# Hash attention and RWKV channel mix on one core: first blocks' differences in three pieces, staged weights scaled ten slots behind their loads

## The chip, the core and the metric

The kernel runs on one core of a Trainium2 chip. A core has engines that run side by side, each working through its own instructions in order: TensorE (PE) multiplies matrices out of SBUF into PSUM, and its weight loads are shown apart as PEld; VectorE (DVE), ScalarE (ACT) and GpSimd (POOL) do elementwise work; SyncE (SP) issues most of the transfers, and POOL and ACT issue a few. Engines wait for each other through semaphores. The metric is the device time of one execution in microseconds (us), as a median over several runs.

## What is computed

Two parts follow each other. First, attention over 4 batches of 8 heads, 768 positions, head size 64, in which a query sees only the keys whose six sign bits (of a projection) equal its own. Its output, heads side by side, is the input x of an RWKV channel mix of width 512 and inner width 1024:

```
q_bits = (einsum('bhsd,dk->bhsk', q, proj) > 0)
k_bits = (einsum('bhsd,dk->bhsk', k, proj) > 0)
mask = q_bucket[:, :, :, None] == k_bucket[:, :, None, :]
scores = where(mask, scale * matmul(q, k.transpose(0, 1, 3, 2)), -1e9)
x = matmul(softmax(scores), v)
x_prev = concatenate([zeros, x[:, :-1, :]], axis=1)
xk = mu_k * x + (1.0 - mu_k) * x_prev
xr = mu_r * x + (1.0 - mu_r) * x_prev
k = maximum(xk @ w_k, 0.0)
v = k * k @ w_v
r = 1.0 / (1.0 + exp(-(xr @ w_r)))
out = r * v
```

## The kernel before

**Pairs and slots.** Heads are taken two at a time: 16 pairs n, four for each batch (NPB is 4). A pair has 12 slots, one for each head j of the two and each of six blocks of 128 keys. One loop over the global slot G (line 605) writes the order of all engines by hand; n and s are the pair and the slot in it. In every slot PE makes one block of scores (`score`, two matmuls at L325), ACT takes the exponential of it (L332), and PE multiplies the block of two slots before with the values (`pv`, L352). After six blocks DVE divides by the row sums (rc at L363, ob at L364).

**What else a pair's slots hold.** `bits` (slot 1): PE's eight sign-bit matmuls for pair n+1 (L287), DVE's signs sg (L291), and eight small SP transfers (L297) that put the bits beside q and k. `turn_out` (slot 3): PE transposes ob of pair n-1 (L378), DVE copies it to a tile xt (L379), and L383 and L384 set the 128 columns ahead of it, which make xt shifted by one position; POOL does these two, except for the last pair of a batch, where DVE does. `mix(b, dc, 0)` (slot 4): DVE makes the difference df of xt and its shifted self (L394), multiplies it by mu_k (L398) and adds the shifted part (L405); the result xk is 128 of the 512 channels of the channel mix's input. `turn` (slots 5, 7, 9 and 11): PE transposes a quarter of q and k of pair n+2 (L269) into a PSUM bank; DVE empties the bank (L272 for q, L274 for k) and casts the lower half (L278), POOL casts the upper half (L277). The quarters of slots 5 and 9 share one bank, with the sign bits of slot 1, and those of slots 7 and 11 the other, with the transposes of slot 3. `values` (slots 6 and 10): POOL casts v of pair n+1 (L305) and sums it (L311 to L315).

**Loads.** In slot 3 SP issues q and k of pair n+3 (L238) and v of pair n+2 (L248). The channel mix's weights come in during pairs 0 to 2 by the table `weights` (line 587). w_k and w_r are loaded by POOL's own transfers (L537), w_r in slot 10 of pairs 1 and 2. w_v is loaded by SP in four blocks of 512 KB (`load_wv`, L544) into a staging pool of two buffers, in slots 0 and 2 of pairs 1 and 2, and POOL scales each block by one half into the bfloat16 weights wv_sb (L550). The third and the fourth block take the buffers of the first and the second.

**Delays.** `later(k, fn)` enters a function that `run_due`, at the head of each slot, runs k slots on. The scale of a block is entered 8 slots behind its load, which puts it at the head of slots 8 and 10 of the same pair.

**The channel mix.** Its matmuls (L424) come from a queue that `ffn` empties little by little between the scores, from slot 5 of pair 4 on for batch 0; the last batch runs alone at the end. It needs all four xk of a batch first, wr_sb later, and wv_sb last.

Of the kernel before, what the change touches and what calls it, by code (L numbers as in the profile page):

```python
# [10 lines left out]
BF16 = mybir.dt.bfloat16  # L11
INT32 = mybir.dt.int32
AF = mybir.ActivationFunctionType
ALU = mybir.AluOpType
AX = mybir.AxisListType

P = 128
# [12 lines left out]
def kernel(  # L30
# [13 lines left out]
    nc = tc.nc  # L44
    B, H, S, D = q.shape
# [5 lines left out]
    NDC = DM // P  # L51
    NFC = DF // P
    NPB = H // 2
# [18 lines left out]
    mu_sb = consts.tile([P, 2 * NDC], FP32, name="mu_sb")  # L72
# [95 lines left out]
    def fast():  # L168
        with ExitStack() as fx:
# [17 lines left out]
            dfp = pool("df", 1)  # L187
            mixp = pool("mix", 2)
# [7 lines left out]
            def bank(which, shape, dt, name):  # L196
                return bkp.tile(shape, dt, name=name, tag=f"bk{which}")
# [16 lines left out]
            def later(k, fn):  # L214
                due.append((clock[0] + k, len(due), fn))

            def run_due():
                ready = sorted(x[:2] for x in due if x[0] <= clock[0])
                for key in ready:
                    fn = next(x for x in due if x[:2] == key)  # L220
                    due.remove(fn)
                    fn[2]()
# [4 lines left out]
            def load_qk(n, split=False, eng=nc.sync):  # L227
                b, t = divmod(n, NPB)
                tag = f"qk{n}" if n < NKEEP else f"qk{n % 3 - 3}"
                tl = nat.tile([P, 2, 2, S // 2], FP32, name=f"qk{n}", tag=tag)  # L230
                nats[n] = tl
                if split:
                    for j in range(2):
                        for (side, i, src), e in zip(SIDES, (nc.sync, nc.scalar)):
                            e.dma_start(out=tl[:, i, j, :], in_=natural(src, b, 2 * t + j))
                else:
                    for side, i, src in SIDES:
                        eng.dma_start(  # L238
                            out=tl[:, i, :, :],
                            in_=src[b, 2 * t : 2 * t + 2].rearrange(  # L240
                                "j (p c) d -> p j (c d)", c=NC_
                            ),
                        )

            def load_v(n):
                b, t = divmod(n, NPB)
                vf = vfp.tile([P, 2, S // 2], FP32, name=f"vf{n}", tag="vf")
                nc.sync.dma_start(  # L248
                    out=vf, in_=v[b, 2 * t : 2 * t + 2].rearrange("j (p c) d -> p j (c d)", c=NC_)
                )  # L250
                vfs[n] = vf
# [134 lines left out]

            mx = {}

            def mix(b, dc, i):
                xt = xts[b, dc]  # L390
                x, xp = xt[:, P : P + S], xt[:, 0:S]
                if i == 0:
                    df = dfp.tile([P, S], BF16, name=f"df{b}_{dc}", tag=f"df{dc}")
                    nc.vector.tensor_tensor(df, x, xp, op=ALU.subtract)  # L394
                    mx["df", b, dc] = df
                nm = ("xk", "xr")[i]
                m = mixp.tile([P, S], BF16, name=f"{nm}{b}_{dc}", tag=f"{nm}{dc}")
                nc.vector.tensor_scalar(  # L398
                    out=m,
                    in0=mx["df", b, dc],  # L400
                    scalar1=mu_sb[:, i * NDC + dc : i * NDC + dc + 1],
                    scalar2=None,
                    op0=ALU.mult,
                )
                nc.vector.tensor_tensor(out=m, in0=m, in1=xp, op=ALU.add)  # L405
                mx[nm, b, dc] = m

            ffbanks = ["C", "D"]
            ffnext = [0]
# [114 lines left out]
            def ffn(amount):  # L524
                if not queue:
                    credit[0] = 0.0
                    return
                credit[0] += amount
                while queue and credit[0] > 0:
                    cost, u = queue.pop(0)  # L530
                    credit[0] -= cost
                    u()


            def load_w(which, c0, nch):
                dst, src = {"k": (wk_sb, moe_w_k), "r": (wr_sb, moe_w_r)}[which]
                nc.gpsimd.dma_start(  # L537
                    out=dst[:, c0 : c0 + nch, :],
                    in_=src[c0 * P : (c0 + nch) * P, :].rearrange("(c p) f -> p c f", p=P),
                )  # L540

            def load_wv(c0):
                st = stg.tile([P, 2, DM], FP32, name=f"wvs{c0}", tag="stg")
                nc.sync.dma_start(  # L544
                    out=st,
                    in_=moe_w_v[c0 * P : (c0 + 2) * P, :].rearrange("(c p) f -> p c f", p=P),
                )
                later(
                    8,
                    lambda: nc.gpsimd.tensor_scalar(  # L550
                        out=wv_sb[:, c0 : c0 + 2, :], in0=st, scalar1=0.5, scalar2=1.0,
                        op0=ALU.mult, op1=ALU.mult,
                    ),
                )
# [9 lines left out]
            for _ in range(22):  # L564
# [10 lines left out]
                out=mu_rows[0:NDC, :], in_=moe_mu_k.rearrange("(c p) -> c p", p=P)  # L575
            )
            nc.sync.dma_start(
                out=mu_rows[NDC : 2 * NDC, :], in_=moe_mu_r.rearrange("(c p) -> c p", p=P)
# [20 lines left out]
            def oo_bank(n, j):  # L599
                return "AC"[j] if n < NPB else "A"  # L600

            def misc_bank(n, s):
                return "BD"[(s // 2) % 2] if n < NPB else "B"

            for G in range(nslots + LAG):
                clock[0] = G
                n, s = divmod(G, 12)
                live = G < nslots
                run_due()

                if live and s == (5 if n == 0 else 3):
                    if n + 3 < NPAIRS:
                        load_qk(n + 3)
                    if n + 2 < NPAIRS:
                        load_v(n + 2)
                w = weights.get(n, {}).get(s)
                if w:
                    if w[0] == "v":
                        load_wv(w[1])
                    else:  # L620
                        load_w(*w)
                old = chunks[G - LAG] if G >= LAG else None
                first = old is not None and old[2] == 0
                if live:
                    score(*chunks[G])
                if old and not first:
                    pv(*old, oo_bank(*old[:2]))
                rate = 25.9 / (NPB * 12 + (3 if n >= NPAIRS - NPB else 0))
                ffn(rate / 2)
                mb = misc_bank(n, s)  # L630
                if live:
                    if n == 0:
                        if s in (0, 1):
                            turn(1, s, 1, "BD"[s])
                    if n == 1 and s == 0:
                        mups = bank(mb, [P, 2 * NDC], FP32, "mups")
                        nc.tensor.transpose(mups, mu_rows, ident32[0 : 2 * NDC, 0 : 2 * NDC])
                        nc.vector.tensor_copy(mu_sb, mups)
                    if s == (3 if n == 0 else 1) and n + 1 < NPAIRS:
                        bits(n + 1, (0, 1), mb)  # L640
                    if s == 3 and n >= 1:
                        turn_out(n - 1, mb)
                    if s == 4 and n >= 1:
                        mix((n - 1) // NPB, (n - 1) % NPB, 0)

                    if n in (NPB, NPB + 1) and G - NPB * 12 in (7, 9, 11, 13):
                        mix(0, (G - NPB * 12 - 7) // 2, 1)
                    if n > NPB and s == 8:
                        mix((n - 1) // NPB, (n - 1) % NPB, 1)
                    if s in (5, 7, 9, 11) and n + 2 < NPAIRS:  # L650
                        x = (s - 5) // 2
                        turn(n + 2, x % 2, x // 2, mb)
                    if s in (6, 10) and n + 1 < NPAIRS:
                        values(n + 1, s // 10)
                    if s in (8, 10) and NKEEP <= n + 1 < NPAIRS:
                        norm(n + 1, (s - 8) // 2)
                ffn(rate / 2)
                if old and first:
                    pv(*old, oo_bank(*old[:2]))
                if live and n >= NPB and n % NPB == 0 and s == MIXSLOT - 1:  # L660
                    queue.extend(ffn_items(n // NPB - 1))

            nm = sgp.tile([P, 1], FP32, name="nm", tag="nm")
# [32 lines left out]
            x = 0  # L696
# [143 lines left out]
    with tc.manual_schedule():  # L840
        fast()
# [33 lines left out]
```

## Time and profile before

| what | value |
|---|---|
| median of 3 runs | 283.14 us (282.72 to 283.64) |
| the profiled execution | 281.45 us |
| its span, first to last instruction | 279.6 us |
| mean granted clock of TensorE | 0.988 |
| busy PE, ACT, DVE, POOL | 262.2, 215.0, 198.6, 113.3 us |
| DVE's sum of waits for POOL's L384 | 6.9 us in 10 waits |
| PE's waits for DVE's L272 | 1.7 us, one wait |

The costliest groups of the page that the change's steps touch or stand beside (operation, its operands and count; then busy time and the mean of one; then the engine's idle time just before, and what ended most of it):

```profile
L332 ACT ACTIVATE pt<-sc,expb 128x768 bf16<-128x768 f32 x192 | 166.5, 904 | 39.4 <-PE sc L325 38.1
L277 POOL CAST aq<-tq 64x384 bf16<-64x384 f32 x32 | 21.1, 658 | 63.3 <-DVE tq L272 63.3
L272 DVE COPY tq<-tpq 128x384 f32<-128x384 f32 x32 | 17.7, 552 | 2.1 <-PE tpq L269 2.0
L384 POOL COPY xt<-xt 128x127 bf16<-128x127 bf16 x12 | 3.6, 302 | 46.4 <-DVE xt L379 46.4
```

And the instructions on the tile wvs (durations are least, median and most, in ns):

```profile
L544 SPq DMA_DIRECT2D wvs<-in_moe_w_v_dram x4: 386/432/578, 24.2 to 42.1; - x4
L550 POOL TENSOR_SCALAR wv_sb<-wvs x4: 1033/1036/1044, 33.4 to 48.0; 128x1024 bf16<-128x1024 f32 x4
```

The duration at L544 is that of issuing a transfer, not of the transfer. An engine that is not the bottleneck loses nothing by standing idle, as POOL does before most of its casts at L277.

### The profile page before, as it was taken

What the parts mean: (1) busy time and instruction counts of PE and PEld (TensorE: products, weight loads), DVE (VectorE), ACT (ScalarE), POOL (GpSimd) and SP (SyncE); (2) the same over time, 40 slices, a digit from 0 to 9 for tenths busy, and PEclk for the clock granted to TensorE, in tenths of its full rate; (3) what the DMA queues carried; (4) which work ended last, traced back from release to release, by engine and by line L of the source; (5) the groups of instructions that cost most, each with busy time, mean ns of one, the idle gap of its engine ahead of it and who ended that gap; (6) DMA issues with size and microseconds to landing.
All of it is one profiled execution on the core that took longest, in us unless ns stands there. A gap on an engine that the chain in (4) does not pass through costs nothing.

```text
span 279.6 us, 6894 instructions
## 1 busy us (share of the span) xinstructions
PE 262.2 (94%) x2530; PEld 165.4 (59%) x2561; DVE 198.6 (71%) x438; ACT 215.0 (77%) x318; POOL 113.3 (41%) x300
## 2 busy tenths in 40 slices
PE   7999997899999999999999999999999889989991
PEld 5466765666565665656565765656565556545540
DVE  3766839879997866769698766769698835576541
ACT  2199995898799896878989896878998898449800
POOL 5885667665554350714455260715444600000000
PEclk9999997999999999999999999999999999999997
DMA  7459597253213050726122040815220001320042
GB/s 231 167 115 208 179 328 248 43 173 101 77 59 117 6 172 4 218 110 191 59 69 108 14 164 7 272 53 166 84 60 4 5 2 39 114 76 2 0 151 86
DMA packets 19896, 29.95 MB, mean 107 GB/s; under 512 B 2184, under 2 KB 15056, under 8 KB 19856
## 3 DMA queue, kind: packets, MB, share of 16 engines
q1 hardware_dynamic: 17928, 25.89, 27.9%
q0 software_dynamic: 1536, 3.15, 5.3%
q8 instruction: 22, 0.36, 0.5%
q10 hardware_dynamic: 392, 0.40, 0.5%
q14 instruction: 18, 0.15, 0.2%
HBM read 24.12 MB, written 6.29 MB: 109 GB/s over the span
## 4 chain that ended last, share of the span: by engine, by line
PE 66%; ACT 9%; DVE 8%; DMA 7%; issue 3%; SPq 3%; POOL 2%; ACTq 0%; DVEq 0%
PE sc L325 15%; PE vp L424 13%; PE kp L424 12%; PE oo L352 8%; ACT pt L332 6%; PE rp L424 5%; DMA wvs<-in_moe_w_v_dram 4%; PE bb L287 4%; PE tpq L269 3%; PE tpk L269 2%; SPq L297 2%; PE ot L378 2%; ACT sq L256 2%; PE oo L343 1%; DMA aq<-sg 1%
## 5 line engine op out<-in xcount | busy, mean ns | idle before, releaser
L332 ACT ACTIVATE pt<-sc,expb 128x768 bf16<-128x768 f32 x192 | 166.5, 904 | 39.4 <-PE sc L325 38.1
L325 PE MATMUL sc<-aq,ak 70*128 70x384 bf16 x384 | 94.9, 328 | 3.2 <-ACT pt L332 0.8
L352 PEld LDWEIGHTS <-pt 128*128 128x128 bf16 x1152 | 61.1, 98 | 26.6 <-issue 0.8
L352 PE MATMUL oo<-va,pt 128*128 128x65 bf16 x1152 | 66.9, 194 | 0.0
L424 PE MATMUL kp<-xk,wk_sb 128*128 128x384 bf16 x256 | 57.7, 325 | 0.8 <-DVE os L487 0.8
L325 PEld LDWEIGHTS <-ak 70*128 70x128 bf16 x384 | 34.9, 98 | 29.3 <-issue 9.1
L424 PE MATMUL vp<-wv_sb,k 128*128 128x512 bf16 (+1 forms) x186 | 50.3, 370 | 0.4 <-issue 0.2
L277 POOL CAST aq<-tq 64x384 bf16<-64x384 f32 x32 | 21.1, 658 | 63.3 <-DVE tq L272 63.3
L455 DVE TENSOR_TENSOR k<-kr 128x384 bf16<-128x384 bf16 x64 | 29.0, 459 | 15.5 <-ACT kr L447 14.3
L424 PEld LDWEIGHTS <-wk_sb 128*128 128x128 bf16 x256 | 22.2, 97 | 13.3 <-issue 4.2
L256 ACT ACTIVATE sq<-qk 128x768 bf16<-128x768 f32 x32 | 27.1, 847 | 0.1
L424 PE MATMUL rp<-wr_sb,xr 128*128 128x512 bf16 x79 | 24.9, 379 | 1.2 <-DVE kr L449 0.8
L424 PEld LDWEIGHTS <-k 128*128 128x128 bf16 x200 | 17.5, 97 | 12.0 <-issue 2.7
L447 ACT ACTIVATE kr<-kp 128x384 bf16<-128x384 f32 x36 | 17.7, 491 | 7.4 <-PE kp L424 7.4
L487 DVE SCALAR_TENSOR_TENSOR os<-th,vp 128x512 f32<-128x512 bf16 (+1 forms) x25 | 16.5, 663 | 9.0 <-PE vp L424 8.9
L384 POOL COPY xt<-xt 128x127 bf16<-128x127 bf16 x12 | 3.6, 302 | 46.4 <-DVE xt L379 46.4
L311 POOL TENSOR_TENSOR s<-vf 128x192 f32<-128x192 f32 x32 | 20.8, 650 | 0.0
L277 POOL CAST ak<-tk 64x384 bf16<-64x384 f32 x32 | 19.3, 602 | 2.4 <-DVE tk L274 2.4
L274 DVE TENSOR_SCALAR tk<-tpk 128x384 f32<-128x384 f32 x32 | 17.6, 550 | 3.4 <-PE tpk L269 3.3
L272 DVE COPY tq<-tpq 128x384 f32<-128x384 f32 x32 | 17.7, 552 | 2.1 <-PE tpq L269 2.0
L269 PE MATMUL tpq<-ident,qk 128*128 128x128 f32 x96 | 16.9, 287 | 2.4 <-DVE tq L272 1.7
L379 DVE COPY xt<-ot 128x768 bf16<-128x768 bf16 x16 | 8.9, 558 | 14.3 <-PE ot L378 14.2
(60 smaller groups left out, 320.0 us busy)
## 6 DMA issues: line engine op xcount, KB each, us to landing
vf<-in_v_dram SPq DMA_DIRECT2D x16, 384.0 KB
out_dram<-os SPq DMA_DIRECT2D x23, 256.0 KB
qk<-in_q_dram SPq DMA_DIRECT2D x13, 384.0 KB
qk<-in_k_dram SPq DMA_DIRECT2D x13, 384.0 KB
wvs<-in_moe_w_v_dram SPq DMA_DIRECT2D x4, 512.0 KB
aq<-sg SPq DMA_DIRECT2D x64, 4.5 KB
wk_sb<-in_moe_w_k_dram POOLq DMA_DIRECT2D x2, 512.0 KB, 5.4
ak<-sg SPq DMA_DIRECT2D x62, 4.5 KB
```

What stands on the lines that cost most here:

```text
L256: nc.scalar.activation(junk, nats[n][:, i].rearrange("p j f -> p (j f)"), AF.Square, accum_out=nrm[:, i, n : n + 1],)
L269: nc.tensor.transpose(tp[:, cols], nats[n][:, i, j, cols], ident32)
L272: nc.vector.tensor_copy(dst, tp)
L274: nc.vector.tensor_scalar(out=dst, in0=tp, scalar1=ALPHA, scalar2=None, op0=ALU.mult)
L277: nc.gpsimd.tensor_copy(au[side, j][0:D, 0:HALF], dst[0:D, :])
L311: nc.gpsimd.tensor_add(s3, vf[:, 0 : 3 * D], vf[:, 3 * D : 6 * D])
L325: nc.tensor.matmul(sc[:, sp, 0:HALF], au["k", j][:, jc * P : (jc + 1) * P], au["q", j][:, sp * HALF : (sp + 1) * HALF], start=True, stop=True,
L332: nc.scalar.activation(pt.rearrange("p (s q) -> p s q", s=2), sc[:, :, 0:HALF], AF.Exp, bias=expb, scale=SCALE,)
L352: nc.tensor.matmul(oo[:, ic, :], pts[n, j, jc][:, ic * P : (ic + 1) * P], vas[n, j][:, jc, :], start=False, stop=(jc == NC_ - 1 and ic == ...
L424: nc.tensor.matmul(box["t"], lhs(), rhs(), start=(i == 0), stop=(i == len(mms) - 1))
L447: nc.scalar.activation(kr, kp, AF.Relu)
L455: 1, lambda: nc.vector.tensor_tensor(out=k2, in0=kr, in1=kr, op=ALU.mult)
```

## The change

There are two edits. `mix` takes a list of steps: step 0 is the difference, step 1 the product with mu, step 2 the sum. For the first three pairs of the first batch, whose mix runs in pairs 1 to 3, the three steps are placed in slots 6, 8 and 10 instead of all three in slot 4; every other call runs all steps at once, where it ran before. And the scale of a staged block of w_v is entered 10 slots behind its load instead of 8, which puts it at the head of slot 10 of the same pair, or of slot 0 of the next.

```
-            def mix(b, dc, i):
+            def mix(b, dc, i, steps=(0, 1, 2)):
                 xt = xts[b, dc]
                 x, xp = xt[:, P : P + S], xt[:, 0:S]
-                if i == 0:
-                    df = dfp.tile([P, S], BF16, name=f"df{b}_{dc}", tag=f"df{dc}")
-                    nc.vector.tensor_tensor(df, x, xp, op=ALU.subtract)
-                    mx["df", b, dc] = df
                 nm = ("xk", "xr")[i]
...
+                for step in steps:
+                    if step == 0 and i == 0:
+                        df = dfp.tile([P, S], BF16, name=f"df{b}_{dc}", tag=f"df{dc}")
+                        nc.vector.tensor_tensor(df, x, xp, op=ALU.subtract)
+                        mx["df", b, dc] = df
+                    if step == 1:
+                        m = mixp.tile([P, S], BF16, name=f"{nm}{b}_{dc}", tag=f"{nm}{dc}")
+                        nc.vector.tensor_scalar(
...
+                        mx[nm, b, dc] = m
+                    if step == 2:
+                        m = mx[nm, b, dc]
+                        nc.vector.tensor_tensor(out=m, in0=m, in1=xp, op=ALU.add)
...
                 later(
-                    8,
+                    10,
                     lambda: nc.gpsimd.tensor_scalar(
...
-                    if s == 4 and n >= 1:
+                    if s == 4 and n >= NPB:
                         mix((n - 1) // NPB, (n - 1) % NPB, 0)
+
+                    if s in (6, 8, 10) and 1 <= n < NPB:
+                        mix(0, n - 1, 0, [s // 2 - 3])
```

In the compiled program the order moves as follows. On DVE, in pairs 1 to 3, L272 and L278 of slot 5 come ahead of the difference; rc, ob, L274 and L278 of slot 7 stand between the difference and the product, and L272 and L278 of slot 9 between the product and the sum. On POOL, the first scale of pairs 1 and 2 stands behind the cast L277 of slot 9 and right before the w_r load's issue, which was behind the second scale before; the second scale stands behind the cast L277 of slot 11, ahead of L383 and L384 of the next pair. The order of SP, PE and ACT does not change.

More of the change, by code (lines that the diff above doesn't have):

```diff
@@ L387, in fast @@
             mx = {}
-            def mix(b, dc, i):
+            def mix(b, dc, i, steps=(0, 1, 2)):
                 xt = xts[b, dc]
                 x, xp = xt[:, P : P + S], xt[:, 0:S]
-                if i == 0:
-                    df = dfp.tile([P, S], BF16, name=f"df{b}_{dc}", tag=f"df{dc}")
-                    nc.vector.tensor_tensor(df, x, xp, op=ALU.subtract)
-                    mx["df", b, dc] = df
                 nm = ("xk", "xr")[i]
[L397 to L406, printed above, removed]
+                for step in steps:
[6 more added lines that the diff above has]
+                        nc.vector.tensor_scalar(
+                            out=m,
+                            in0=mx["df", b, dc],
+                            scalar1=mu_sb[:, i * NDC + dc : i * NDC + dc + 1],
+                            scalar2=None,
+                            op0=ALU.mult,
+                        )
+                        mx[nm, b, dc] = m
+                    if step == 2:
+                        m = mx[nm, b, dc]
+                        nc.vector.tensor_tensor(out=m, in0=m, in1=xp, op=ALU.add)
             ffbanks = ["C", "D"]
```

## The prediction

> **What bounds the kernel now.** I read first the page's slices, for where the busy engines let go.
>
> ```profile
> PE   7999997899999999999999999999999889989991
> DVE  3766839879997866769698766769698835576541
> ACT  2199995898799896878989896878998898449800
> PEclk9999997999999999999999999999999999999997
> ```
>
> A slice is 7.0 us. From 7 us on PE is at nine tenths or more, and ACT close to it, with one hole that all rows share: the seventh slice (42 to 49 us), where ACT falls to 5 and the granted clock to 7. The hole lies in the part that the change edits, so next I cut the trace by head pairs, from one pair's eight sign-bit matmuls (L287) to the next pair's: pairs 1, 2 and 3.
>
> ```profile
> core 0: us, PE busy (x) PEld busy (x) DVE busy (x) ACT busy (x) POOL busy (x), PEclk, DMA share, GB/s
> 24.06:34.62 10.56, 10.03 (x128) 6.98 (x125) 7.94 (x17) 9.72 (x13) 5.59 (x15) 1.00 0.74 217
> 34.62:47.85 13.23, 11.32 (x127) 7.92 (x124) 8.17 (x18) 10.09 (x14) 8.94 (x22) 0.87 0.93 296
> 47.85:58.72 10.87, 9.97 (x128) 6.93 (x125) 9.57 (x18) 9.71 (x13) 8.38 (x24) 1.00 0.28 53
> ```
>
> The same work (128 matmul rows, some records missing) takes 10.56, 13.23 and 10.87 us: pair 2 is 2.67 us long. The chain of waits says why. Its columns are start, duration, piece.
>
> ```profile
> 24.17 7.82 DMA wvs<-in_moe_w_v_dram
> ...
> 32.70 4.00 DMA wvs<-in_moe_w_v_dram
> ...
> 36.78 1.04 POOL wv_sb L550
> 37.82 0.71 POOL wr_sb L537
> ...
> 40.96 0.24 POOL xt L384
> ...
> 41.23 0.57 DVE df L394
> ...
> 43.36 0.55 PE tpq L269 x3
> ...
> 46.85 3.06 DVE ak L278
> ...
> 50.66 0.51 PE ot L378 x6
> ```
>
> The second staged block of value weights is issued at 32.70 and lands at 36.70. POOL came to scale it at 34.98 and stood. Behind that on POOL are a load's issue, the value sums, a cast, and then the one-column shift L384 of the pair's block xt, which DVE's difference L394 needs. DVE stood too, and behind L394 on DVE is the copy L272 that empties the PSUM bank in which PE wants the next transpose. So PE stood. The waits between 34 and 50 us give the three prices (total, times, longest):
>
> ```profile
> DVE df L394 <- POOL xt L384: 3.5, 1, 3.5
> PE tpq L269 <- DVE tq L272: 1.7, 1, 1.7
> POOL wv_sb L550 <- DMA wvs<-in_moe_w_v_dram: 1.8, 1, 1.8
> ```
>
> **The change, part by part.** No operation is added or removed: the compiled instruction counts of all engines agree, and only places in order move.
>
> *Scales two slots later (POOL).* Walk POOL's order for pair 2 with the trace's durations. The ak cast ends at 33.38. The aq cast now comes first (0.50), then the first scale (1.04), the issue of the wr load (0.77), the value chain (1.89, from 38.54 to 40.43), a cast (0.44), the second scale (1.04), and memset and shift (0.3). These add to 5.98, so the shift ends near 39.4 instead of 41.20. The second scale begins near 38.0, 1.3 us after its block landed: the 1.79 us wait is gone.
>
> *The difference in three pieces (DVE).* L394 moves from slot 4 to slot 6, behind the transpose copy of slot 5. PE's transpose ran at 38.25. Its copy starts 0.56 later (as 31.33 to 31.89 one pair earlier), takes 0.55, the cast 0.35, so DVE reaches L394 at about 39.75, after the shift's 39.4. The bank is empty at 39.4, and PE asks for it again at 41.44 (the place that pair 1 gives it, 0.50 behind the start of the score matmul at 40.94): no wait. The other two pieces, 0.42 and 0.56, fall into slots 8 and 10, where pair 1 shows DVE idle 0.35 and 0.44 ahead of L272 and L274. They lie beside PE's work; without that cover they would cost PE up to their 0.98.
>
> *What PE gets back.* The transpose at 43.36 comes at 41.44: 1.92 us. From there to the next sign bits took 4.49 (43.36 to 47.85), against 3.29 in pair 1 (31.33 to 34.62) and 3.29 in pair 3 (55.43 to 58.72). The clock in the windows of 1 us from 44 to 48 was granted at 0.55, 0.50, 0.50 and 0.74. That is another 1.20, and pair 2 gives 3.12.
>
> The Trainium skill ("TensorE: Matmul & The Clock Gate", section "What's actually happening") has the clock halve only after an idle window of about 3.4 us; here a hole of under 2 us came just before the half clock. By that rule the hole need not be the cause and the gain would stop at 1.92; by the row it is 3.12, and I go by the row.
>
> *Pair 3.* PE waits 0.66 for DVE's ob before the transposes at 50.66, because DVE's cast L278 took 3.06 instead of 0.35: it began while POOL ran two scales, a cast and a load issue without a gap (46.52 to 49.76), and ended 0.15 after them. In the new order the cast L277 and the scale are no longer followed by a second scale, and DVE's cast comes near 44.15, beside one scale (43.6 to 44.6) and the issue (to 45.4). Pair 3's 10.87 would fall to between 10.56 (pair 1) and 10.11 (pair 2 with its hole taken out: 13.23 - 3.12). That is 0.31 to 0.76; I take 0.45, the nearer to pair 1.
>
> *Pair 1.* PE idles 0.28 before the transpose at 28.14, put down to DVE's difference, which no longer stands there; but the compiled program has this matmul wait for its q load as well (issued at 22.48, with the DMA engines full from 24 to 30 us). Bounds 0 to 0.45 (28.14 against 27.69, 0.51 behind its score matmul as in pair 2). I take 0.
>
> *Costs.* (a) The wr load's issue comes 2.9 us earlier (34.95 against 37.82), into the loads of the next q, k and v. Moved bytes from 33 us on put k's landing at about 37.8; at half the rate from 36.4 it would be 39.2, and PE wants it at 39.83. Cost 0, at worst about 0.7 if it comes 1.3 later still. (b) The cast L278 at 34.06, which waited for one scale (0.57 in all), now meets a scale from 33.9 on with the issue right behind: at worst 35.8 instead of 34.63. The sign bits' SP DMAs would then start 1.1 later (37.2), and after them the eight small ones at 0.7 us each, the last staged block and the next q and k, which have about 1.5 us to spare. Cost 0 to 0.5. (c) SP's issues of staged blocks three and four wait for the scales of one and two: 34.95 against an issue at 34.78 (0.2 late, with the sign bits behind it not due before 36.12), and 39.1 against 42.10 (free). (d) The last scale finds its block in time: issued at 42.10, all loads landed by 48.4, and wanted near 47.8. If POOL waits, what stands behind it is pair 3's shift, wanted only at 49.9. Together I take 0.3 for (a) to (d), bounds 0 and 1.2.
>
> The Trainium skill ("SBUF — State Buffer", section "Who interferes with whom") speaks against this change: a VectorE copy, cast or scalar multiply in its two-port mode and a GpSimd instruction exclude each other for a whole instruction. More such pieces now lie between POOL's work. By the rule each of six moved pieces could wait for one POOL instruction (up to 1.04 in this trace); the row of 3.06 is longer than any one instruction, and the rows at slots 8 and 10 of pair 3 (0.44 and 0.74 instead of 0.35) are shorter.
>
> **Sum.** 3.12 + 0.45 + 0 - 0.3 = 3.27 us off the profiled execution, 281.45 (span 279.6 and 1.85 around it), giving 278.2. From 60 us on the order is the same and PE and ACT are dense, so what arrives early stays early. The median of the runs is 283.14, 1.7 above the profiled one; less 3.27 it is 279.9.
>
> **The rivals.**
> 1. *The hole closes only in part.* PE gets the 1.92 but not the 1.20, because another short hole brings the low clock anyway, and the costs reach 1.2: 1.92 - 1.2 = 0.7 off, or 282.4; with 0.3 of cost, 281.5. For it: pair 2 keeps DMA share 0.93. Against it: no other hole of PE between 20 and 60 us is over 0.7, and none of those lowered the clock.
> 2. *POOL's gapless run shuts DVE out (slower).* Without the wait, POOL is busy from 31.2 to 39.4 with no gap. If the cast L278 at 34.06 is held to the end of that run, as the 3.06 one was, it ends at 39.5; then rc, ob (0.8), and PE's transposes of ob start at 40.4 instead of 36.60: 3.8 lost, and 1.20 of clock behind it, 5.0 against the 3.57 gained: 1.4 slower, 284.6. It decides against the change once the cast ends after about 38.1. For it: the 3.06 row. Against it: that hold ended with the load's issue and not with POOL's run, and the cast at 34.06 got in after one scale although POOL went on with a cast.
> 3. *The moved load makes the next wait.* The wr load, issued 2.9 us earlier, holds up pair 2's k until 41.7 instead of 37.8; PE, which wants it at 39.83, stands 1.9 and pays the 1.20 of clock again: 3.27 - 3.1 = 0.2 off, 283.0, no change. For it: DMA share 0.98 to 1.19 from 35 to 41 us. Against it: k is queued ahead of 0.9 MB (v and a staged block) that had all landed by 42, so one load of 256 KB would have to cost it nearly four us.
>
> That the change doesn't do what it says, and POOL stands for the staged block all the same, is a rival to the cause more than to the time. With the shift at 41.2 and the difference in slot 6, DVE runs L394 (0.56), rc and ob (0.8) and the slot-7 copy (0.55) to 43.1, where PE wants that bank at 43.0 (1.58 after 41.44, as in pair 1): 0.1 lost. The other way round, scales moved and the difference left whole in slot 4: 39.4 + 1.52 + 0.55 = 41.5 against 41.44, again 0.1. By these rows either half of the change gives nearly all of it.
>
> **How the numbers follow.** Forecast 0.70 (own range 278.8 with all upper bounds, 3.12 + 0.76 + 0.45 = 4.33 off, to 281.0), rival 1 0.12, rival 2 0.10, rival 3 0.08. A measurement of this kernel can tell 0.3% or 0.85 us, so faster means below 282.3 and slower above 284.0. Faster: 0.70, and most of rival 1 (0.09): 0.79. Within: the rest of rival 1, rival 3 and a little of rival 2: 0.12. Slower: 0.09. The range from 278.7 to 282.3 leaves out rivals 2 and 3 and the tail of 1.
>
> **What would show it.** Right: no POOL wait for wvs at L550 in pairs 1 and 2; no DVE wait for POOL's shift above 0.5 us; transpose of pair 2's ninth slot within 0.6 of 41.4; granted clock 1.00 from 42 to 49; pair 2 at 10.1 to 10.6. Wrong: a cast L278 over 1.5 us before 40 us, a PE wait for a q or k load near 39.8 or 48 to 50, or a clock below 1.00 between 30 and 60 us.

## The result, and the profile after

| | before | after |
|---|---|---|
| median | 283.14 us (11 runs, 282.19 to 284.09) | 280.56 us (11 runs, 279.77 to 282.24) |
| ratio, 95% interval | | 0.9912 (0.9892 to 0.9933) |
| the profiled execution, span | 281.45, 279.6 | 280.56, 278.7 |

The change makes the kernel faster by 0.7 to 1.1%, 2.6 us by the medians, where 3.3 were forecast. On another chip (run e7 below) it was 0.9958 (0.9937 to 0.9979), 1.1 us. The two profiled executions differ by 0.9 us only, because that of before lay 1.7 below its median. Medians are over all runs of a kernel, while the ratios leave out runs more than 1.5% above the fastest of the same kernel, so that the two need not agree to the tenth.

The hole is gone. The page's slices of the changed kernel:

```profile
PE   7798999999899999999999999999999889989990
DVE  3766879789996866769597866769696826576550
ACT  2198977998799987968899896969998897359700
PEclk9999999999999999999999999999999999999997
```

The seventh slice of ACT is back at 7 and the granted clock holds. ACT's sixth slice is no longer full, though (7, where it was 9), and the same cut by head pairs shows that not all of the gain arrived:

```profile
core 0: us, PE busy (x) PEld busy (x) DVE busy (x) ACT busy (x) POOL busy (x), PEclk, DMA share, GB/s
24.47:34.68 10.21, 9.96 (x128) 7.04 (x125) 7.53 (x15) 9.73 (x13) 5.58 (x13) 1.00 0.79 240
34.68:45.88 11.20, 10.65 (x128) 7.11 (x125) 9.51 (x18) 9.67 (x13) 9.29 (x22) 1.00 0.70 206
45.88:57.10 11.22, 10.66 (x128) 7.12 (x125) 9.49 (x19) 9.68 (x13) 9.29 (x24) 1.00 0.61 183
```

Pair 2 went from 13.23 to 11.20, pair 3 rose from 10.87 to 11.22. The waits between 34 and 50 us name the new limit. None is for wvs or for the shift L384 any more:

```profile
ACT pt L332 <- PE sc L325: 3.1, 2, 1.5
PEld bb L287 <- DVE tk L274: 1.9, 2, 1.0
```

The sign bits L287 now wait for DVE's last copy L274. What makes it late is no row of waits but one long busy bar. DVE's and POOL's timelines (start, duration, then the instruction):

```profile
33.05 0.36 DVE L278 CAST aq<-tq 64x384 bf16<-64x384 f32 x1
33.42 1.84 DVE L410 TENSOR_TENSOR xk<-xk,xt 128x768 bf16<-128x768 bf16 x1
35.18 0.55 DVE L274 TENSOR_SCALAR tk<-tpk 128x384 f32<-128x384 f32 x1
```

```profile
33.08 0.69 POOL L277 CAST aq<-tq 64x384 bf16<-64x384 f32 x1 [0.17 <-DVE tq L272]
33.76 1.04 POOL L554 TENSOR_SCALAR wv_sb<-wvs 128x1024 bf16<-128x1024 f32 x1
34.76 0.78 POOL L541 DMA_DIRECT2D wr_sb<-in_moe_w_r_dram  x1
```

The third piece of the difference, the sum L410, is 0.56 long in the kernel before, where it is line 405:

```profile
42.27 0.56 DVE L405 TENSOR_TENSOR xk<-xk,xt 128x768 bf16<-128x768 bf16 x1
```

Here it starts beside POOL's cast and ends at 35.26, 0.46 behind the end of the scale (34.80): all but 0.1 of its 0.56 us of work fits behind the scale, so that it did next to nothing while POOL's cast and scale ran, and the trace shows that as DVE being busy. The text calls this a hold. The copy L274, wanted at about 33.5 when the last transpose is done, runs at 35.18, the last two of the eight sign-bit matmuls start at 35.78 and 36.13 (the first at 34.68), and ACT stands 1.53. The same happens one pair later (1.84 again, at 44.63).

The Trainium skill ("SBUF — State Buffer", section "Who interferes with whom") says that a VectorE instruction with two SBUF inputs contends with a GpSimd instruction that reads SBUF, and that issue order decides which of the two waits. Beside the cast, which started 0.34 before the sum, the trace agrees. Beside the scale it does not: by the starts in the profile the scale came 0.34 after the sum (33.76 and 33.42) and ran ahead of it all the same. The prediction weighed this rule and priced it too low; it named copies, casts and scalar multiplies, and the sum is of the other form.

Rows of the whole that make up the profiled difference: the pairs 1 to 3 give 2.03 (34.66 to 32.63); 0.41 is lost ahead of pair 1, 0.29 in pair 6 (16.16 against 15.87) and 0.4 between the last DVE instruction and the end.

### The profile page after: what moved, and what is told of

It is laid out like the page before. It is cut to its first block, busy times and chain, and to the rows that moved or that the text cites. A ratio compares the mean times of both kernels' runs of the same rounds, so it can differ in the third digit from the quotient of the medians.

```text
span 278.7 us, 6896 instructions
## 1 busy us (share of the span) xinstructions
PE 260.8 (94%) x2530; PEld 164.0 (59%) x2561; DVE 199.7 (72%) x438; ACT 214.9 (77%) x318; POOL 115.0 (41%) x300
## 4 chain that ended last, share of the span: by engine, by line
PE 63%; ACT 14%; DVE 12%; DMA 4%; issue 4%; ACTq 0%; SPq 0%; POOL 0%; DVEq 0%
PE sc L325 15%; PE vp L428 13%; PE kp L428 12%; ACT pt L332 11%; PE oo L352 7%; PE rp L428 4%; PE bb L287 4%; DMA qk<-in_k_dram 3%; PE tpq L269 2%; ACT sq L256 2%; PE tpk L269 2%; DVE xk L410 2%; PE ot L378 2%; DVE tq L272 2%; DMA vf<-in_v_dram 1%
## 5 line engine op out<-in xcount | busy, mean ns | idle before, releaser
L325 PE MATMUL sc<-aq,ak 70*128 70x384 bf16 x384 | 93.9, 325 | 3.5 <-ACT pt L332 1.3
L277 POOL CAST aq<-tq 64x384 bf16<-64x384 f32 x32 | 21.4, 670 | 60.7 <-DVE tq L272 60.7
L384 POOL COPY xt<-xt 128x127 bf16<-128x127 bf16 x12 | 3.6, 302 | 46.5 <-DVE xt L379 46.5
L272 DVE COPY tq<-tpq 128x384 f32<-128x384 f32 x32 | 17.7, 552 | 5.1 <-PE tpq L269 5.0
L277 POOL CAST ak<-tk 64x384 bf16<-64x384 f32 x32 | 19.0, 595 | 4.1 <-DVE tk L274 4.1
L274 DVE TENSOR_SCALAR tk<-tpk 128x384 f32<-128x384 f32 x32 | 17.6, 549 | 3.7 <-PE tpk L269 3.7
L364 DVE TENSOR_TENSOR ob<-oo,rc 128x384 bf16<-128x384 f32 x32 | 17.8, 558 | 1.1
```

Source lines behind the costliest of these rows:

```text
L272: nc.vector.tensor_copy(dst, tp)
L274: nc.vector.tensor_scalar(out=dst, in0=tp, scalar1=ALPHA, scalar2=None, op0=ALU.mult)
L277: nc.gpsimd.tensor_copy(au[side, j][0:D, 0:HALF], dst[0:D, :])
L325: nc.tensor.matmul(sc[:, sp, 0:HALF], au["k", j][:, jc * P : (jc + 1) * P], au["q", j][:, sp * HALF : (sp + 1) * HALF], start=True, stop=True,
L364: nc.vector.tensor_tensor(out=obs[n][:, :, j * D : (j + 1) * D], in0=oo[:, :, 0:D], in1=rc.to_broadcast([P, NC_, D]), op=ALU.mult,)
```

## The experiments

Theory A: the removed wait is the gain, and what is missing is DVE's sum standing beside POOL's scale in slot 10. Theory B: the late scale itself, with the w_r load's issue behind it, holds what the sign bits need, whatever DVE does there. The first measure of a run is the time from the first sign-bit matmul of one pair to that of the next; a late copy falls into the next pair's length, so pair 4 is listed too.

| kernel | pair 1 | 2 | 3 | 4 | sum | median, us | ratio to before, 95% |
|---|---|---|---|---|---|---|---|
| before | 10.56 | 13.23 | 10.87 | 14.39 | 49.05 | | |
| the change | 10.21 | 11.20 | 11.22 | 14.40 | 47.03 | 280.56 | 0.9912 (0.9892 to 0.9933) |
| e7, the change again | 10.76 | 11.20 | 11.21 | 14.41 | 47.58 | 281.63 | 0.9958 (0.9937 to 0.9979) |
| e1, scales alone | 10.57 | 10.27 | 11.44 | 14.67 | 46.95 | 280.28 | 0.9920 (0.9887 to 0.9953) |
| e2, pieces alone | 10.26 | 11.55 | 11.74 | 14.40 | 47.95 | 282.49 | 0.9955 (0.9927 to 0.9983) |
| e3, sum in slot 8 | 10.53 | 10.12 | 10.45 | 15.11 | 46.21 | 279.65 | 0.9890 (0.9854 to 0.9926) |
| e4, sum in slot 2 | 10.61 | 10.18 | 10.51 | 14.40 | 45.70 | 279.67 | 0.9893 (0.9857 to 0.9929) |
| e8, the same | 10.30 | 10.12 | 10.94 | 14.40 | 45.76 | 279.01 | 0.9854 (0.9828 to 0.9880) |
| e12, the same | 10.49 | 10.12 | 14.29 | 14.39 | 49.29 | 279.09 | 0.9876 (0.9839 to 0.9913) |
| e5, scales 11 slots | 10.66 | 10.12 | 11.14 | 14.39 | 46.31 | 281.77 | 0.9951 (0.9927 to 0.9975) |
| e6, scales in halves | 10.59 | 10.22 | 11.56 | 14.61 | 46.98 | 280.55, one execution | |
| e11, second scale alone | 10.57 | 10.65 | 12.76 | 14.66 | 48.64 | 283.07 | 1.0008 (0.9982 to 1.0035) |
| e9, all in slot 6 | 10.45 | 10.93 | 10.74 | 14.94 | 47.06 | 280.08 | 0.9901 (0.9866 to 0.9937) |
| e10, slot 2 and halves | 10.59 | 10.12 | 10.96 | 15.16 | 46.83 | 279.86 | 0.9893 (0.9859 to 0.9927) |

Before's medians beside them: 283.14 for the change; 282.39 for e1 to e4; 282.77 for e5 to e8; 282.83 for e9 to e12. The pairs are of one execution, the ratios of many. The profiled execution of e12 took 282.3, far above its median of 279.09; its pairs are listed but not compared, and what made its third pair long is told below.

**e1, the scales alone.**

```
-                    8,
+                    10,
```

in `load_wv` of the kernel before, with `mix` untouched.

> Only the scales move (10 slots behind their loads); the difference stays whole in slot 4. Theory A (in the changed kernel DVE's sum L410 of slot 10 is held for 1.3 us by POOL's scale, 1.84 instead of 0.56, and with it the copy L274 and the sign bits of the next pair): no DVE sum stands beside a scale here, so from sign bits to sign bits pairs 2 and 3 take 10.2 to 10.7 us each instead of 11.20 and 11.22, the shift L384 of pair 2 ends 1.8 us earlier than before the change, and the time is 279.0 to 280.0. Theory B (the late scales and the w_r load's issue right behind them hold DVE's casts and so the sign bits, whatever DVE does in slot 10): pairs 2 and 3 take about 11.2 as in the changed kernel, and the time is 280.6 or more.

Pair 2 took 10.27: the hole closed with this one number. Pair 3 took 11.44, above both expectations, and for another reason than B's. With the whole difference in slot 4, DVE waited 2.9 us for pair 3's shift, though POOL did not wait for any load: its run up to the shift is simply long. PE then stood 0.54 for the copy L272, and 0.42 for a q load. A's range of 279.0 to 280.0 was missed by 0.3 (280.28; the interval is 279.2 to 281.1, which takes in B's 280.6 as well). So the time does not decide between the theories here.

**e2, the pieces alone.** The changed kernel with the 8 of before.

> Only the difference goes in pieces (slots 6, 8, 10); the scales stay 8 slots behind their loads. Both theories: POOL stands about 1.8 us for the second staged block again, but the copy of slot 5 no longer stands behind the difference, so PE has no hole over 1 us and the clock stays at 1.00 in pair 2. Theory A: the first scale still runs while the sum of slot 10 wants to start (33.4 in both kernels), so the sum is long again (over 1.2 us) in at least one pair, and the time is 280 to 281.5. Theory B: the scales are out of the way of slot 10's casts, sign bits on time, pairs 2 and 3 take 10.2 to 10.7, and the time is near 279.0.

POOL stood 2.23 for the second block, and no PE hole over 1 us came of it: the pieces took that wait off PE's path, as the prediction had it. But pairs 2 and 3 took 11.55 and 11.74. A's detail was wrong and its mechanism right: not the sum (0.76 in all three pairs) but the instruction that happened to stand beside a scale was held, at two of the four scales: the cast L278 (1.10) and the product L400:

```profile
44.11 1.58 DVE L400 TENSOR_SCALAR xk<-df,mu_sb 128x768 bf16<-128x768 bf16 x1
44.44 1.03 POOL L554 TENSOR_SCALAR wv_sb<-wvs 128x1024 bf16<-128x1024 f32 x1
```

Beside the fourth scale it was the other way round. The cast, the sum and the scale stand as in the changed kernel, and the sum again starts 0.34 behind the cast, but here the sum went first and the scale took 1.35 instead of 1.04:

```profile
46.22 0.69 POOL L277 CAST aq<-tq 64x384 bf16<-64x384 f32 x1 [0.74 <-DVE tq L272]
46.56 0.76 DVE L410 TENSOR_TENSOR xk<-xk,xt 128x768 bf16<-128x768 bf16 x1
46.88 1.35 POOL L554 TENSOR_SCALAR wv_sb<-wvs 128x1024 bf16<-128x1024 f32 x1
```

B's 279.0 is excluded: the interval, times before's median of 282.39, ends at 280.3 on its low side. A's 280 to 281.5 is met by the ratio (281.1) and missed by the median, 282.49, which is no lower than before's.

**e3 and e4, the sum somewhere else.** e3 draws it ahead to slot 8; e4 puts it off to slot 2 of the next pair (the edit of e4):

```
-                    if s in (6, 8, 10) and 1 <= n < NPB:
+                    if s in (6, 8) and 1 <= n < NPB:
                         mix(0, n - 1, 0, [s // 2 - 3])
+                    if s == 2 and 2 <= n <= NPB:
+                        mix(0, n - 2, 0, [2])
```

> The changed kernel with the sum L410 drawn ahead from slot 10 to slot 8, right behind the product; scales as in the changed kernel. Theory A: the sum runs in 0.6 to 0.8 us ahead of the scale, the copy L274 and the sign bits are on time, pairs 2 and 3 take 10.2 to 10.6 instead of 11.2, ACT's holes of 1.5 us at the sign bits shrink to about 0.45, and the time is 278.0 to 279.2. Theory B: sign bits late as before, pairs 2 and 3 at 11.2, time 280.6 within 0.3%.

> The changed kernel with the sum L410 put off from slot 10 to slot 2 of the next pair, where DVE waits for PE's transposes; scales as in the changed kernel. Theory A: as with the sum in slot 8, 278.0 to 279.2, with the sum at 0.56 to 0.9. Theory B: 280.6 within 0.3%, pairs 2 and 3 at 11.2. If the cast L278 of slot 11 is held by the scale in the sum's place (up to 1.1 us), the sign bits are still on time, since they read the copy and not the cast, and only the division of the row sums is later.

By the pairs both do as A has it: 10.12 and 10.45, 10.18 and 10.51. The scale now meets the cast L278 of slot 11, which is held (1.0 to 1.2), but the copy L274 stands ahead of it in DVE's order. e4's pairs, and DVE beside the first scale (POOL 33.87 to 34.91):

```profile
34.80:44.98 10.18, 9.84 (x127) 6.86 (x124) 8.66 (x17) 9.54 (x13) 8.37 (x21) 1.00 0.77 225
44.98:55.49 10.51, 10.18 (x127) 7.11 (x124) 9.46 (x19) 9.96 (x13) 9.89 (x24) 1.00 0.73 202
```

```profile
33.65 0.56 DVE L274 TENSOR_SCALAR tk<-tpk 128x384 f32<-128x384 f32 x1
34.24 0.99 DVE L278 CAST ak<-tk 64x384 bf16<-64x384 f32 x1
```

A hold costs nothing there: the sign bits read the copy, and only the division of the row sums comes later. B fell with these pair lengths. The medians, 279.65 and 279.67, miss A's 278.0 to 279.2 by 0.5, and their intervals (278.3 to 280.4 together) reach into B's range, so that the time decided only later, in e7 and e8.

A hold needs no scale. In pair 2 of e4 the difference L396 took 1.80, beside POOL's casts and value sums alone:

```profile
40.03 1.80 DVE L396 TENSOR_TENSOR df<-xt 128x768 bf16<-128x768 bf16 x1
```

The pair still took 10.18: the copy that stands behind L396, that of slot 7, empties a bank which PE wants again only in slot 11. In e3 such a hold did cost something: L396 took 1.28 in pair 3, DVE had no gap from there to the copy L274 of slot 11 (55.78), and the last two sign-bit matmuls came at 56.38 and 56.73, the first at 55.65. That is its 15.11 in pair 4.

**e7 and e8, the changed kernel and e4 on one chip.**

> The changed kernel once more, on the same chip and beside the same runs of before as the kernel with the sum in slot 2. Theory A: 0.985 to 0.993 of before, the sum L410 of pairs 1 and 2 held by the scale (over 1.5 us) in the profiled execution again, pairs 2 and 3 at 11.0 to 11.4 us. If the hold was chance in one execution, the sum is under 1 us here and the pairs take 10.2 to 10.6.

> The sum L410 in slot 2 of the next pair, scales as in the changed kernel: the same kernel as in the first four, now beside the changed one. Theory A: faster than the changed kernel by 0.7 to 1.8 us, pairs 2 and 3 at 10.1 to 10.6. Theory B: the same as the changed kernel within 0.3%.

The sum of e7 took 1.84 in both pairs again, to the hundredth; pairs 2 and 3 took 11.20 and 11.21. It is not chance. e8 is 0.9854 of before and the change 0.9958, with intervals that don't touch: moving the one instruction is worth 2.6 us by the medians (281.63 to 279.01), more than the 0.7 to 1.8 expected. The pairs of the two profiled executions account for 1.8 of it (47.58 and 45.76); the rest is not traced. e7's ratio, 0.9958, lies above the expected range.

**e5, the scales one slot later still.**

```
-                    10,
+                    11,
```

> The changed kernel with the scales 11 slots behind their loads instead of 10, the sum left in slot 10. The first scale then stands on POOL behind the value sums of slot 10 and 2.6 us later. Theory A: the sum of slot 10 meets the value sums alone (each 0.6 or less) and takes 0.9 or less, the copy L274 and the sign bits are on time, pairs 2 and 3 take 10.2 to 10.7, time about 1 us below the changed kernel's. Theory B: the scale later still brings sign bits as late or later, pairs at 11.2 or more, time the same or longer.

The sum took 0.76, the sign bits were on time, and pair 2 took 10.12: A's mechanism. The time did not follow (281.77, runs from 279.06 to 284.65). SP's queue of waits shows the price:

```profile
SPq L548 <- POOL wv_sb L554: 3.1, 1, 3.1
```

The third staged block waits in SP's queue for the buffer of the first, 3.1 us, and is issued at 37.24 instead of 34.82; the q, k and v loads behind it start no later than in the changed kernel (q at 44.08 and 44.45). PE waited 0.6 for a k load in pair 3 (11.14). What makes the other executions longer was not traced.

**e6, halves.** Each scale as two instructions of 512 columns.

> The changed kernel with each scale in two instructions of 512 columns right behind each other. If a DVE instruction waits for one POOL instruction and gets in at the next boundary, the sum L410 waits for one half less and takes about 1.3 instead of 1.84 us. If it waits until POOL's run of port-using instructions lets go, it stays at 1.8 or more. One look: only durations are read from it.

Neither: the sum took 0.87 in both pairs. The first half, 1.01 instead of 0.61, waited for the sum. So here DVE got in when POOL's cast ended, and in the changed kernel, with whole scales, POOL's next instruction did, four times of four. Which of the two goes first at such a border is open, since in e2 DVE did against a whole scale. The expectation for e10 takes this run as letting DVE in between the halves; the durations don't show that. Pair 3 took 11.56 although the sum was short: L396 had taken 1.80 in pair 2 (40.70), DVE had no gap from there on, and the copy for the sign bits was late again (46.28).

**e11, the second block alone.** This asks whether the wait of 1.79 us, by itself, was the lost time.

```
-                    8,
+                    10 if c0 == 2 else 8,
```

> The kernel before with one thing moved: only the second staged block is scaled 10 slots behind its load, the other three stay at 8, and the difference stays whole in slot 4. Theory (the 1.79 us wait of POOL for that block opened the hole of PE, and the hole brought the half clock): no wait for wvs at L550, no hole of PE over 1 us in pair 2, granted clock 1.00 from 42 to 49 us, pair 2 at 10.1 to 10.7 instead of 13.23, and 2 to 3 us off the time. Rival (the clock falls of itself there, as the load of pairs 2 and 3 has it): clock below 0.9 somewhere from 40 to 50 us, pair 2 at 11.2 or more.

Pair 2 took 10.65, as the theory has it, and the time did not change: 1.0008. The wait had moved to the fourth block, one pair later. The waits from 45 to 59 us repeat those of before to the tenth, but for DVE's, which was 3.5:

```profile
DVE df L394 <- POOL xt L384: 4.2, 1, 4.2
...
PEld tpq L269 <- DVE tq L272: 1.9, 1, 1.9
POOL wv_sb L550 <- DMA wvs<-in_moe_w_v_dram: 1.8, 1, 1.8
PE tpq L269 <- DVE tq L272: 1.8, 1, 1.8
```

POOL came to that block at 46.6 instead of 47.98, and SP issued it at 44.39 instead of 42.10, so the block that had landed in time before is now late (pair 3: 12.76). Moving one scale is not enough; moving two or three was not tried. The rival on the clock falls in this execution, in a way that the theory did not expect either: a hole of 1.79 us in PE, and the granted clock stayed at 1.00 in every window of 1 us from 53 to 60.

**e12, e9 and e10.** e12 is e4 once more. e9 runs the three steps whole in slot 6 (`if s == 6 and 1 <= n < NPB: mix(0, n - 1, 0)`), e10 is e4 with halves.

> The sum L410 in slot 2 of the next pair, as in two runs before: 0.983 to 0.991 of before, pairs 2 and 3 at 10.1 to 10.9. Beside it stand the next two kernels on the same chip.

> Scales 10 slots behind their loads, and difference, product and sum together in slot 6, not in pieces. If what counts is only that none of them stands beside the scale and that the shift has time until slot 6, this equals the kernel with the sum in slot 2 within 0.3%, with the three at 0.4 to 1.3 us each ahead of rc and ob of slot 7. If the pieces as such are needed, 1.5 us at one place hold back the copy L274 of slot 7, PE waits for its bank in slot 11, and pairs 2 and 3 take 11 us or more.

> The sum in slot 2 of the next pair, and each scale in two halves of 512 columns. The halves let a waiting DVE instruction in at their boundary (seen once: the sum took 0.87 instead of 1.84 beside them). Holds of the cast L278 of slot 11 shrink from 1.0 or 1.2 to 0.8 or less; pairs 2 and 3 at 10.1 to 10.6, time equal to the kernel with whole scales or up to 0.5 us less. If halves cost POOL more than they free DVE (1.2 to 1.6 us for a pair of them instead of 1.04), the same within 0.3%.

e12: the ratio, 0.9876, is as expected. In the profiled execution pair 2 took 10.12, but in pair 3 PE waited 2.49 us for a k load (from 50.95), the granted clock was 0.50 from 55 to 58 us, and the pair took 14.29. In the same kernel's e4 and e8 PE waited for a load for 0.3 and 0.7 us. Whether the earlier w_r load makes such a wait more likely was not tested.

e9: the second reading, in small. PE waited 1.1 us in two waits for the copy of slot 7 in its bank, pairs 2 and 3 took 10.93 and 10.74, and the median lies 1.0 above e12's (280.08 and 279.09), though the intervals overlap. That reading's "11 us or more" was not reached. L396 was held here too (1.28 in pair 2), and part of the wait may be due to that.

e10: the holds of L278 of slot 11 shrank to 0.55 and 0.77 and pair 2 took 10.12. But the cast L278 of slot 5 in pair 3 met the first of two halves, and was held through the second and through POOL's next instructions, up to a cast that ended at 52.06:

```profile
49.98 2.36 DVE L278 CAST aq<-tq 64x384 bf16<-64x384 f32 x1
```

DVE had no gap from there to the copy for the sign bits (56.10): pair 3 took 10.96 and pair 4 15.16. No gain over whole scales can be told (279.86 and 279.09, intervals overlapping).

e4 is the version with the most evidence for it, in three comparisons: 0.9893, 0.9854 and 0.9876 of before, 2.7 to 3.8 us by the medians. e3 (0.9890) and e10 (0.9893) can't be told from it.

## Why the prediction was right, and where it was off

The direction, the range (278.7 to 282.3) and the mechanism by which the hole closes held; the gain was 2.6 and not 3.3, and 1.1 in e7.

- *The chain from the staged block to PE.* Right. POOL does not wait for wvs, the second scale starts at 37.91 (38.0 forecast), the shift ends at 39.23 (39.4), L396 waits for nothing, the clock is 1.00 from 42 to 49 us. The transpose of pair 2's ninth slot came at 42.59 instead of 41.44, because the last two sign-bit matmuls of slot 1 came late: from the first of the eight on it is 7.91 (42.59 less 34.68) against 6.82 forecast. So two of the signs of being right were missed, that transpose within 0.6 of 41.4 and pair 2 at 10.1 to 10.6 (11.20), both by the hold that the next point tells of.
- *"The other two pieces ... fall into slots 8 and 10 ... They lie beside PE's work."* This is the step that failed. The cover was DVE's idle time before L274; what was not looked at is what POOL does at that moment, and the other half of the change had just put the scale there. The sum cost not 0 but 1.28 each (1.84 less 0.56), in two pairs. Against the forecast lengths, pair 2 is 1.09 longer (11.20, 10.11) and pair 3 0.80 (11.22, 10.42): 1.9 us, where the costs had been given 0.3 with a bound of 1.2. Pair 1's 0.35 made up some of it. e3, e4 and e8, beside e7, show it: move the sum and the pairs take 10.1 to 10.9. e5 shows it from the other side: move the scale, and the sum takes 0.76 and pair 2 10.12.
- *The hold as a price.* The prediction let POOL hold a piece for one instruction at most, six pieces in all, and then set it aside for the rows of 0.44 and 0.74. Those rows were from places without a scale beside them, and the price by the rule, up to 1.04 for a piece, was below the 1.28 that the sum lost.
- *"By these rows either half of the change gives nearly all of it."* Half right. The scales alone give as much as both (0.9920 beside 0.9912 and 0.9958); the pieces alone give 0.9955, and nothing by the median (282.49 beside 282.39), because the scales of slot 8 then hold DVE.
- *The clock's 1.20.* Taken from one row and given as certain. The profiled execution of e11 has a hole of the same size without it. That execution is not typical, though: each run has its mean granted clock on record, and it is 0.990 or less in 10 of the 12 runs of e11 and 0.992 in this one. For before it is 0.990 or less in 49 of 67 runs on three chips, for the changed kernel in 3 of 21 (on the chip of e7, 15 of 21 and 3 of 10). So most executions of before lost some clock that most of the changed kernel kept; where in the execution is not on record.
- *Rival 3, the wr load in front of k.* No such wait in the changed kernel; in e12, where the load stands at the same place, PE did wait 2.49 for k, one pair later than the rival has it. *Rival 2, DVE shut out for POOL's whole run.* Its mechanism came true in small, on the sum instead of the cast: a hold of 1.84 instead of the 4.0 us (34.06 to 38.1) from which it would have decided. *Rival 1* (0.7 to 1.6 off) comes close to the two profiled executions, 0.9 apart, but not by its cause: the clock was regained.
- *The shift to the median.* The 3.27 were taken off an execution 1.7 below its own median. The medians differ by 2.6 on one chip and 1.1 on another, the profiled pairs by 2.0: the forecast was too high by a quarter at least. That the median came within 0.7 of the forecast is in part luck: the profiled execution of the changed kernel took 280.56, where 278.2 had been worked out.

## What to carry to other kernels

When an instruction of VectorE is moved into an idle place, look at what POOL runs at that place: VectorE and GpSimd can hold each other, and the trace shows the hold as busy time and not as a wait. If a hold can't be avoided, order the engine so that the instruction that PE needs stands ahead of the one that is held. And a wait that was removed in one of several equal places can turn up in the next with the same size, as in e11: look at all of them, and measure again.

## What was not expected of the hardware

- The hold is repeatable to 10 ns (1.84 at four places in two executions), and yet the instructions alone do not decide who goes first: with the same cast, sum and scale at about the same distances, DVE went first in e2 (sum 0.76, scale 1.35), as it did against scales of 512 columns (0.87, two of two). What decides is open.
- A hole of PE of 1.79 us left the granted clock at 1.00 (e11), while one of 1.75 us before the change was followed by three windows of 1 us at 0.50 to 0.55 and one at 0.74, and one of 2.49 us (e12) by three at 0.50. So near 1.8 us the length of the hole alone does not decide it.
